# Block-sparse attention, expert attention and an MLP in one kernel: the same instructions in another order of issue, with other PSUM banks

## Chip, core and metric

The kernel runs on one core of one Trainium2 chip. The metric is the device time of one execution in microseconds, lower is better. Every program here computes the same outputs from the same inputs.

## The reference

Three stages follow each other, in fp32. The first is attention on q, k, v of shape (2, 8, 768, 64). Each query sees the keys within 16 positions, and besides them 24 block keys (the maximum over each block of 32 keys) with block values (the mean over the block):

```python
k_sum = k.reshape(B, H, nb, block, D).max(axis=3)
v_sum = v.reshape(B, H, nb, block, D).mean(axis=3)
scores_l = scale * np.matmul(q, k.transpose(0, 1, 3, 2))
mask_l = np.abs(pos[:, None] - pos[None, :]) < window
scores_s = scale * np.einsum('bhsd,bhnd->bhsn', q, k_sum) + np.log(block)
scores_all = np.concatenate([np.where(mask_l, scores_l, -1e9), scores_s], axis=-1)
return softmax(scores_all) @ np.concatenate([v, v_sum], axis=2)
```

Its output, as x of shape (2, 768, 512), goes into a mixer of four experts. Each expert is a causal attention head of width 64 with its own output matrix, and each token adds up its two best experts, weighted by a softmax over their two gate logits:

```python
for e in range(E):
    q, k, v = x @ wq[e], x @ wk[e], x @ wv[e]
    a = softmax(causal(scale * (q @ k.transpose(0, 2, 1))))
    out += gate[e] * (a @ v @ wo[e])
```

The third stage mixes tokens by two matrices of rank 32 and ends with an MLP, 512 to 2048 to 512, and a residual:

```python
u = x + (x.transpose(0, 2, 1) @ U @ V).transpose(0, 2, 1)
return u + np.maximum(u @ w_ch1, 0.0) @ w_ch2
```

## The kernel before

**Tiling.** The 16 heads form eight pairs (numbered 0 to 7), and each pair has three *slots* of 256 queries, 24 slots in all. A slot runs through four steps on TensorE: the scores (L410), the transposes of the exponentials (L421), the weighted sum over V (L433) and the transposes of the result (L448), with VectorE (DVE), ScalarE (ACT) and GpSimd (POOL) between them. For each pair SP loads K (L310), two halves of q (L313) and V (L357). POOL writes scaled copies of K and of the block maxima into the score operands (`kcopy`, L398) and casts the block sums of V into V's tile (`vcast`, L246); DVE takes the maxima over blocks of K (`kmax`, L381); TensorE adds up the blocks of V (`vsum`, L364). There are three q buffers and three V buffers, taken by the pair's number modulo 3, and two K buffers, taken modulo 2. In the rows `ex`, `pt_77` and `w1h_85` are the q buffers 0, 1 and 2; `a_86` holds the raw K; `pt_78` with `c_79` is the score operand 0, `w1h_82` with `w1l_83` the score operand 1; `vb` and `w1l_84` hold V; `vs` are the block sums of V and `ks` the block maxima of K.

The mixer's projections (L594, L645), its scores (L676), its transposes (L709) and its sums (L727) follow, first for batch 0 while attention of batch 1 still runs. The products of the mixer and the MLP are made of three matmuls, of a high and a low part of each operand. The MLP of batch 0 (L961, L974) and of batch 1 (L901, L933) stands at the end, from about 200 us on.

**Warm-up.** 37 matmuls of zeros (`wake_up`, L331) are spread over the beginning: most ahead of the first real work, the others between its steps. Each is recorded as two matmuls in the profile, as are all matmuls of fp32.

**What sets the order.** Nothing of the order is found at run time. Each piece of work (a load, a copy, the scores of a slot, ...) is registered as a *unit* by `at` (L1002), and a unit may have several parts, one after the other (for the scores: the matmuls, then the row minimum on DVE, then the exponentials on ACT). A table `TIMES` (from L48) gives a rank, 0 to 1925, to every part of the 783 units. A loop at the end of the kernel takes the parts by rank and issues their instructions, and each engine, SP's queue of loads among them, works through its own instructions in the order of issue. A second table, `BANKS`, gives a unit the PSUM bank (one of eight) that it writes:

```python
return BANKS[part] if BANKS else i                       # bank_of
...
t, u, i, fn, args = heapq.heappop(todo)
part_now[0] = u
part = fn(*args) if callable(fn) else fn
wait = next(part, None) if isinstance(part, GeneratorType) else None
if wait is not None:
    heapq.heappush(todo, (TIMES[u][i + 1] if TIMES else t + wait, u, i + 1, part, ()))
```

An instruction that has to wait for another engine, or for a buffer or a bank to come free, holds up all that stands behind it on its own engine. On SP this goes for loads into a buffer that is still read: the load, and every load behind it, is issued once the readers are done.

Of the kernel before, what the change touches and what calls it, by code (L numbers as in the profile page):

```python
# [35 lines left out]
def f(ap):  # L36
# [12 lines left out]
    (67,), (107,), (84,), (3,), (52,), (39,), (41,), (80,), (119,), (8,), (42,), (56,), (36,), (220,), (159,), (44,),  # L49
    (179,), (75,), (48,), (106,), (47,), (2,), (1,), (6,), (40,), (477,), (49,), (9,), (22,), (66,), (21,), (76,),  # L50
    (37,), (65,), (74,), (4,), (24,), (138,), (27,), (26,), (16,), (43,), (12,), (14,), (20,), (15,), (57,), (86,),
    (32,), (112,), (0,), (77, 79, 92), (101, 114), (122, 129), (140, 149, 155), (83, 90, 94), (98, 116), (124, 130),
    (139, 144, 165), (89, 91, 109), (110, 111), (127, 143), (148, 164, 167), (113, 115, 126), (128, 142), (154, 166),
    (193, 202, 212), (117, 125, 136), (150, 153), (173, 180), (195, 201, 209), (118, 123, 133), (145, 151),
    (156, 188), (204, 221, 256), (170, 172, 185), (194, 210), (217, 230), (241, 252, 282), (161, 169, 174),
    (183, 198), (229, 250), (251, 258, 293), (176, 184, 190), (200, 205), (228, 254), (275, 284, 302),
    (207, 213, 218), (226, 240), (261, 265), (279, 289, 306), (211, 225, 232), (253, 255), (269, 276),
    (288, 297, 309), (208, 219, 234), (243, 248), (273, 286), (298, 299, 316), (259, 264, 266), (291, 294),
    (304, 313), (333, 340, 354), (263, 267, 281), (287, 292), (301, 325), (335, 336, 356), (277, 290, 305),
    (311, 320), (327, 329), (337, 351, 362), (307, 314, 317), (363, 378), (380, 388), (397, 411, 421),  # L60
    (310, 324, 345), (408, 422), (433, 440), (446, 471, 476), (328, 331, 341), (366, 371), (382, 399),
    (405, 423, 425), (367, 379, 394), (418, 427), (444, 450), (454, 464, 467), (368, 387, 401), (413, 426),
    (445, 453), (455, 463, 473), (376, 384, 389), (415, 432), (435, 457), (533, 534, 549), (430, 438, 451),
    (461, 479), (484, 486), (516, 520, 536), (439, 449, 458), (474, 481), (485, 498), (521, 527, 537),
    (436, 442, 456), (483, 500), (512, 543), (547, 608, 612), (17,), (13,), (58,), (11,), (50,), (23,), (10,), (28,),
    (46,), (19,), (38,), (34,), (29,), (51,), (54,), (55,), (33,), (69,), (18,), (64,), (78, 85, 88), (97,), (104,),
    (103,), (93,), (5,), (7,), (45,), (31,), (30,), (62,), (25,), (53,), (60,), (71,), (61,), (63,), (70,), (59,),
    (87,), (96, 102, 105), (132,), (121,), (35,), (73,), (81,), (72,), (108,), (99,), (134,), (131,), (160,), (137,),
    (146,), (135, 141, 152), (186,), (175,), (82,), (120,), (158,), (100,), (168,), (171,), (182,), (178,), (181,),
    (189,), (197,), (177, 187, 196), (235,), (247,), (147,), (157,), (95,), (162,), (192,), (199,), (223,), (245,),  # L70
    (236,), (216,), (203,), (233, 239, 260), (296,), (280,), (191,), (215,), (231,), (206,), (249,), (283,), (278,),
    (272,), (262,), (285,), (268,), (319, 322, 334), (375,), (364,), (224,), (246,), (271,), (242,), (326,), (312,),
    (365,), (348,), (339,), (330,), (350,), (318, 323, 342), (419,), (385,), (270,), (308,), (355,), (274,), (357,),
    (349,), (400,), (392,), (381,), (343,), (377,), (383, 391, 396), (420,), (424,), (315,), (369,), (410,), (352,),
    (237, 257, 300), (238, 303, 332), (163, 214, 227), (295, 321, 338), (344, 373, 374), (346, 359, 361),
    (390, 395, 402), (347, 353, 360), (358, 370, 372), (386, 393, 398), (403, 404, 407, 412, 414, 417, 429, 431, 493),
    (68,), (406, 409, 416, 434, 437, 459, 469), (428, 441, 443, 447, 448, 465, 470), (222,), (244,), (480, 482, 494),
    (487, 490, 495), (499, 501, 514, 529), (594, 599), (541, 554), (567, 571), (489, 503, 506), (505, 511, 515),
    (522, 535, 550, 551), (556, 557), (502, 513, 517), (492, 507, 525), (526, 552, 564, 566), (574, 577), (572, 580),
    (452, 462, 466, 468, 475, 497, 508), (460, 472, 478, 488, 496, 504, 509), (519, 523, 538), (528, 540, 542),  # L80
# [1181 lines left out]
```

## Time and profile before

| | us |
|---|---|
| median of three runs (428.94, 429.00, 430.14) | 429.0 |
| the profiled execution | 429.18 |
| its span, from the first instruction to the last | 427.4 |
| TensorE busy | 419.6 (98%) |
| DVE busy | 296.1 (69%) |
| ACT busy | 244.8 (57%) |
| POOL busy | 202.9 (47%) |

The busy time of an engine says how much of the span it worked, not who waited for whom. That is to be read from the rows of single stretches: each row has the start of a group of instructions, how long the group took, and in square brackets the idle time before it with what ended that time. PE is TensorE, SPq the queue of SP, which issues the loads. The granted clock of TensorE is 1.00 in all stretches.

### The profile page before, as it was taken

To read this page: it belongs to the slowest core of one execution; us is meant where nothing else is said; L and a number is where in the kernel's file an instruction comes from. 1 tells how busy PE (TensorE), PEld (TensorE's weight loads), DVE (VectorE), ACT (ScalarE), POOL (GpSimd) and SP (SyncE) were. 2 spreads that over 40 slices of the span, in tenths; PEclk is the share of its full clock that TensorE was granted. 3 is DMA by queue.
4 is the path that set the end of the run, shared out by engine and by line. 5 is a ranking of instruction groups with operands and counts; after the bars stand their busy time and mean duration, and the time that the engine had idled before them with its cause. 6 is when DMAs were issued, how large, how long until landed. Compare 5 with 4: busy or idle time off the path is not lost.

```text
span 427.4 us, 9539 instructions
## 1 busy us (share of the span) xinstructions
PE 419.6 (98%) x3594; PEld 386.6 (90%) x3594; DVE 296.1 (69%) x784; ACT 244.8 (57%) x623; POOL 202.9 (47%) x286
## 2 busy tenths in 40 slices
PE   8899999999999999999999999999999999999995
PEld 8789889999989988978888898998889999999995
DVE  4688856776758766669778467666659876755664
ACT  6669856567766778886465453443453554434341
POOL 6799893368785877832254443434543132000000
PEclk9999999999999999999999999999999999999999
DMA  8989850000112013511346234231103000000001
GB/s 215 219 234 248 220 119 2 5 0 20 44 62 64 2 49 100 196 41 61 92 156 200 97 123 123 75 123 51 50 26 123 2 2 0 26 28 0 26 26 49
DMA packets 14925, 35.24 MB, mean 82 GB/s; under 512 B 2080, under 2 KB 3616, under 8 KB 14880
## 3 DMA queue, kind: packets, MB, share of 16 engines
q1 hardware_dynamic: 14880, 34.64, 27.2%
q8 instruction: 28, 0.46, 0.5%
q14 instruction: 17, 0.14, 0.1%
HBM read 31.49 MB, written 3.15 MB: 81 GB/s over the span
## 4 chain that ended last, share of the span: by engine, by line
PE 94%; DMA 2%; SPq 1%; DVE 1%; issue 0%; POOL 0%; DVEq 0%; ACT 0%; POOLq 0%
PE ps L974 16%; PE ps L933 13%; PE ps L901 8%; PE ps L961 8%; PE ps L645 8%; PE ps L524 5%; PE ps L676 5%; PE ps L410 4%; PE ps L594 4%; PE ps L727 4%; PE ps L709 4%; PE ps L983 4%; PE ps L433 3%; PE ps L421 3%; DMA vb<-in_vW_dram 2%; PE ps L448 1%
## 5 line engine op out<-in xcount | busy, mean ns | idle before, releaser
L246 POOL TENSOR_SCALAR a<-a 64x384 fp32r<-64x384 f32 x64 | 33.4, 523 | 19.4 <-ACT a L650 10.2
L966 ACT ACTIVATE a<-ps 128x384 fp32r<-128x384 f32 x32 | 15.6, 491 | 40.2 <-PE ps L961 36.5
L961 PE MATMUL ps<-x,w1h 128*128 128x384 f32 x128 | 37.6, 339 | 0.0
L901 PE MATMUL ps<-x,w1h 128*128 128x256 f32 x192 | 37.2, 282 | 0.0
L645 PE MATMUL ps<-x,m 128*128 128x384 f32 x192 | 37.1, 342 | 0.0
L645 PEld LDWEIGHTS ps<-x,m 128*128 128x128 f32 x192 | 33.0, 188 | 0.1
L968 DVE SCALAR_TENSOR_TENSOR a<-ps,a 128x384 fp32r<-128x384 f32 x32 | 17.7, 553 | 19.9 <-ACT a L966 19.8
L901 PEld LDWEIGHTS ps<-x,w1h 128*128 128x128 f32 x192 | 30.8, 189 | 0.1
L700 POOL TENSOR_SCALAR ex<-ex,rs,gate 128x256 f32<-128x256 f32 (+5 forms) x36 | 24.9, 699 | 6.8 <-DVE nmx L684 2.6
L676 PE MATMUL ps<-a 128*128 128x384 f32 (+4 forms) x128 | 27.7, 337 | 0.0
L687 ACT ACTIVATE ex<-ex,nmx 128x256 f32<-128x256 f32 (+5 forms) x36 | 23.4, 651 | 7.1 <-DVE nmx L684 5.9
L901 PE MATMUL ps<-x,w1l 128*128 128x256 f32 x96 | 27.1, 282 | 0.0
L974 PE MATMUL ps<-m,a 128*128 128x512 f32 x108 | 26.8, 393 | 0.0
L249 DVE TENSOR_TENSOR x<-x,x 128x384 fp32r<-128x384 f32 (+1 forms) x28 | 17.7, 639 | 12.3 <-ACT x L908 9.8
L263 DVE TENSOR_SCALAR x<-x 128x256 uint32<-128x256 uint32 (+3 forms) x38 | 20.3, 541 | 8.0 <-DMA x<-in_w_dram 6.9
L684 DVE CUSTOM_DVE_ANT_0 ex<-ps,cc 128x256 f32<-128x256 f32 (+5 forms) x36 | 20.8, 598 | 6.6 <-PE ps L676 2.7
L267 DVE SCALAR_TENSOR_TENSOR x<-x 128x256 uint32<-128x256 uint32 (+3 forms) x38 | 22.9, 614 | 3.3 <-ACT x L265 3.1
L961 PEld LDWEIGHTS ps<-x,w1h 128*128 128x128 f32 x128 | 23.6, 188 | 1.4 <-issue 0.4
L974 PEld LDWEIGHTS ps<-m,a 128*128 128x128 f32 x108 | 20.0, 188 | 3.7
L265 ACT ACTIVATE x<-x 128x256 f32<-128x256 f32 (+3 forms) x38 | 20.6, 554 | 3.5 <-DMA x<-in_w_dram 3.5
L717 ACT COPY pt<-ps 128x384 f32<-128x384 f32 (+1 forms) x40 | 19.9, 519 | 4.2 <-PE ps L709 4.0
L249 DVE TENSOR_TENSOR a<-a,a 128x384 fp32r<-128x384 f32 (+1 forms) x24 | 15.6, 657 | 8.9 <-ACT a L918 4.8
(317 smaller groups left out, 1236.2 us busy)
## 6 DMA issues: line engine op xcount, KB each, us to landing
x<-in_w_dram SPq DMA_DIRECT2D x16, 512.0 KB, 3.6
x<-in_w_dram SPq DMA_DIRECT2D x20, 256.0 KB, 2.9
vb<-in_vW_dram SPq DMA_DIRECT2D x5, 585.0 KB, 5.8
a<-in_kP_dram SPq DMA_DIRECT2D x7, 416.0 KB, 6.4
out_dram<-a SPq DMA_DIRECT2D x11, 256.0 KB, 2.0
x<-in_wm_dram SPq DMA_DIRECT2D x4, 386.0 KB, 6.2
tb<-in_w_dram SPq DMA_DIRECT2D x6, 256.0 KB, 3.1
a<-in_w_dram SPq DMA_DIRECT2D x6, 256.0 KB, 3.1
```

Of the source, the lines that this page charges most:

```text
L246: pool.tensor_scalar(dst, src, 1.0, 0.0, op0=ALU.mult, op1=ALU.add)
L249: dve.tensor_tensor(dst, src, f(hi), op=ALU.subtract)
L267: dve.scalar_tensor_tensor(low, high, 3, low, op0=ALU.logical_shift_left, op1=ALU.bitwise_or)
L524: pe.matmul(acc, wo[k][:, int(a == 2), 128 * c:128 * c + 128], w[k][:, int(a == 1)], start=j == 0, stop=j == 11)
L645: pe.matmul(acc, (WML if wl else WMH)[k][:, 128 * e:128 * e + 128], xt(b, k, xl)[:, c], start=n == 0, stop=n == 11)
L676: pe.matmul(flat[:, base + c0:base + c1], QS[u][:, 128 * i:128 * i + 128], kk[:, c0:c1], start=x == 0, stop=x == 1)
L687: act.activation(ex[:, 0:W], ex[:, 0:W], AF.Exp, bias=nmx, scale=-1.0, accum_out=sums)
L700: pool.tensor_scalar(ex, ex, rs[:, i % 2:i % 2 + 1], gate[b][:, i, e:e + 1], op0=ALU.mult, op1=ALU.mult)
L901: pe.matmul(acc[:, 256 * i:256 * i + 256], (W1L if wl else W1H)[q][:, c, 128 * (ff % 2):128 * (ff % 2) + 128], cp(1, c, xl)[:, o], start=m ...
L933: pe.matmul(acc[:, 256 * hf:256 * hf + 256], v[:, BLK[a]], w[wl], start=g < 2 and q == 0 and hf == 0 and i == 0, stop=q == 7 and i == 2, s ...
L961: pe.matmul(acc, (W1L if wl else W1H)[ff // 2][:, c, 128 * (ff % 2):128 * (ff % 2) + 128], cp(b, c, xl)[:, o], start=n == 0, stop=n == 5)
L974: pe.matmul(out_bank(b, 3 * j + t), a[:, 128 * t:128 * t + 128], w, start=False, stop=ff == 15 and x == 2, skip_group_check=True)
```

## The change

Only the numbers in the two tables change. The units, their parts, the instructions and the lines of the code are the same; 771 of the 783 entries of `TIMES` have other ranks, and 266 units have another bank. So on each engine the same instructions stand in another order, and the matmuls write other banks.

```diff
 TIMES = [
-    (67,), (107,), (84,), (3,), (52,), (39,), (41,), (80,), (119,), (8,), (42,), (56,), (36,), (220,), (159,), (44,),
...
+    (63,), (42,), (88,), (3,), (32,), (54,), (11,), (39,), (24,), (10,), (22,), (47,), (43,), (189,), (71,), (51,),
...
 BANKS = [
-    -1, -1, -1, -1, 3, 5, 1, 0, 0, 0, 7, 5, 2, 3, 3, 0, 3, 4, 4, 2, 4, -1, -1, -1, -1, -1, -1, -1, -1, -1, -1, -1, -1,
...
+    -1, -1, -1, -1, 0, 1, 3, 6, 3, 2, 3, 3, 0, 2, 1, 5, 7, 5, 7, 6, 6, -1, -1, -1, -1, -1, -1, -1, -1, -1, -1, -1, -1,
```

The start on TensorE, as a difference of the two orders (- before, + now): warm-up matmuls (L331), the block sums of V of pair 0 (L364) and the scores of slot 0 (L410).

```order
@@ -1,9 +1,9 @@
 L1257 UNCONDITIONAL_BRANCH
-L331 MATMUL ps<-vst 128x128 x29
+L331 MATMUL ps<-vst 128x128 x30
+L364 MATMUL ps<-vb,cc 32x128 x12
 L410 MATMUL ps<-pt_78,ex 64x120 x2
 L410 MATMUL ps<-c_79,ex 64x120 x2
...
-L364 MATMUL ps<-vb,cc 32x128 x12
 L331 MATMUL ps<-vst 128x128 x2
```

The block sums of V of pair 0 have moved from behind the scores of slot 0 to ahead of them, and one warm-up matmul from behind them to the start.

The loads on SP before, from the last pieces of pair 0 on. Row 14 is V of pair 1, rows 13 and 11 the last q of pair 0, row 15 the two q halves of pair 1, rows 16 and 20 K of pairs 2 and 3, rows 19 and 22 the two q halves of pair 2, rows 17 and 21 those of pair 3.

```order
12 L357 DMA vb<-in_vW_dram 96x780
13 L313 DMA ex<-in_qT_dram 64x512
14 L357 DMA vb<-in_vW_dram 96x1560
15 L313 DMA pt_77<-in_qT_dram 64x768 x2
16 L310 DMA a_86<-in_kP_dram 128x832
17 L313 DMA ex<-in_qT_dram 64x768
18 L357 DMA w1l_84<-in_vW_dram 96x1560
19 L313 DMA w1h_85<-in_qT_dram 64x768
20 L310 DMA a_86<-in_kP_dram 128x832
21 L313 DMA ex<-in_qT_dram 64x768
22 L313 DMA w1h_85<-in_qT_dram 64x768
23 L357 DMA vb<-in_vW_dram 96x1560
```

The same place of the new order. Row 14 is V of pair 1, rows 13 and 15 the q halves of pair 1, rows 17 and 22 those of pair 2, rows 21 and 23 those of pair 4.

```order
12 L313 DMA ex<-in_qT_dram 64x512
13 L313 DMA pt_77<-in_qT_dram 64x768
14 L357 DMA vb<-in_vW_dram 96x1560
15 L313 DMA pt_77<-in_qT_dram 64x768
16 L310 DMA a_86<-in_kP_dram 128x832
17 L313 DMA w1h_85<-in_qT_dram 64x768
18 L357 DMA w1l_84<-in_vW_dram 96x1560
19 L313 DMA ex<-in_qT_dram 64x768
20 L310 DMA a_86<-in_kP_dram 128x832
21 L313 DMA pt_77<-in_qT_dram 64x768
22 L313 DMA w1h_85<-in_qT_dram 64x768
23 L313 DMA pt_77<-in_qT_dram 64x768
```

A q half of pair 1 now stands ahead of V of pair 1, and a q half of pair 4 ahead of the second q half of pair 2; the second q half of pair 3 (row 21 before) has moved to behind K of pair 4. Further on, both q halves of pair 5 now stand ahead of a load of mixer weights and of V of pairs 5 and 6; before, one of them stood behind V of pair 5 and the other behind K of pair 6.

POOL before, from the first casts of V's block sums (pair 0) on. Rows 30, 35, 37 and 38 are copies for pair 2.

```order
28 L246 TENSOR_SCALAR vb<-vs 24x8x64
29 L246 TENSOR_SCALAR vb<-vs 24x4x64
30 L398 TENSOR_SCALAR pt_78<-a_86 64x12x64
31 L246 TENSOR_SCALAR vb<-vs 24x8x64
32 L246 TENSOR_SCALAR vb<-vs 24x4x64
33 L246 TENSOR_SCALAR w1h_85<-cc 64x768
34 L246 TENSOR_SCALAR vb<-vs 24x12x64
35 L398 TENSOR_SCALAR pt_78<-ks 64x12x24
36 L246 TENSOR_SCALAR vb<-vs 24x12x64
37 L398 TENSOR_SCALAR pt_78<-a_86 64x12x32
38 L398 TENSOR_SCALAR c_79<-a_86 64x12x32
```

The same place of the new order:

```order
27 L246 TENSOR_SCALAR vb<-vs 24x4x64
28 L246 TENSOR_SCALAR vb<-vs 24x8x64
29 L246 TENSOR_SCALAR vb<-vs 24x4x64
30 L246 TENSOR_SCALAR vb<-vs 24x8x64
31 L246 TENSOR_SCALAR w1h_85<-cc 64x768
32 L246 TENSOR_SCALAR vb<-vs 24x12x64
33 L398 TENSOR_SCALAR c_79<-ks 64x12x24
34 L246 TENSOR_SCALAR vb<-vs 24x12x64
35 L398 TENSOR_SCALAR pt_78<-a_86 64x12x32
36 L398 TENSOR_SCALAR pt_78<-ks 64x12x24
37 L398 TENSOR_SCALAR c_79<-a_86 64x12x32
```

All four casts for pair 0 now stand together, with no copy for pair 2 among them, and the first copy for pair 2 is one of the block maxima.

## Rows read from the trace of the kernel before

**Rows 1.** The page: busy time, share and instructions of each engine; the instruction queue.

```profile
PE 419.6 (98%) x3594; PEld 386.6 (90%) x3594; DVE 296.1 (69%) x784; ACT 244.8 (57%) x623; POOL 202.9 (47%) x286
...
q8 instruction: 28, 0.46, 0.5%
```

**Rows 2.** TensorE by stretch: us, busy us (records), granted clock, DMA share, GB/s.

```profile
0.00:60.00 60.00, 56.66 (x897) 1.00 0.89 224
60.00:200.00 140.00, 139.89 (x1235) 1.00 0.15 49
200.00:424.00 224.00, 223.08 (x1466) 1.00 0.19 64
```

**Rows 3.** Chain of waits behind 200 us: start, us, what.

```profile
272.32 1.05 PE ps L961 x6
```

**Rows 4.** Timeline of all engines, first 18 us.

```profile
7.52 0.58 SPq L357 DMA_DIRECT2D vb<-in_vW_dram  x1
...
9.93 0.43 PE L410 MATMUL ps<-pt,ex 128*64 128x120 f32 x4 [0.44 <-ACT pt L341]
...
12.17 0.86 PE L364 MATMUL ps<-vb,cc 96*32 96x128 f32 x24 [1.20 <-issue]
```

**Rows 5.** Timeline of TensorE, 15 to 32 us.

```profile
15.52 0.87 PE L364 MATMUL ps<-vb,cc 96*32 96x128 f32 x24
...
16.81 0.60 PE L421 MATMUL ps<-cc,woh 128*120 128x128 f32 x4
17.25 0.39 PE L331 MATMUL ps<-vst 128*128 128x128 f32 x2
17.47 0.83 PE L421 MATMUL ps<-cc,pt 128*120 128x128 f32 x4
...
20.84 0.71 PE L331 MATMUL ps<-vst 128*128 128x128 f32 x4
21.48 1.15 PE L433 MATMUL ps<-vb,w1h 120*64 120x65 f32 x32
...
27.18 0.49 PE L331 MATMUL ps<-vst 128*128 128x128 f32 x2
27.59 0.43 PE L410 MATMUL ps<-pt,w1h 128*64 128x120 f32 x4
```

**Rows 6.** Timeline of POOL, 10 to 46 us.

```profile
18.87 0.83 POOL L398 TENSOR_SCALAR pt<-a 64x768 f32<-64x768 f32 x1 [2.27 <-DMA a<-in_kP_dram]
...
26.66 0.83 POOL L398 TENSOR_SCALAR c<-a 64x768 f32<-64x768 f32 x1
```

**Rows 7.** Timeline of DVE, first 19 us.

```profile
18.66 0.95 DVE L381 TENSOR_REDUCE ks<-a 128x24 f32<-128x768 f32 x1 [0.85 <-DMA a<-in_kP_dram]
```

**Rows 8.** DMA from 0 to 60 us; loads issued at 18.75, 27.51, 40.49 (KB, us to landing).

```profile
DMA packets 5050, 13.41 MB, mean 224 GB/s; under 512 B 976, under 2 KB 1616, under 8 KB 5040
...
w1h<-in_qT_dram SPq DMA_DIRECT2D x1, 192.0 KB, 7.3
...
a<-in_kP_dram SPq DMA_DIRECT2D x1, 416.0 KB, 4.3
...
w1h<-in_qT_dram SPq DMA_DIRECT2D x1, 192.0 KB, 8.1
```

**Rows 9.** Timeline of TensorE, 32 to 56 us.

```profile
33.85 0.43 PE L410 MATMUL ps<-w1h,ex 128*64 128x120 f32 x4
...
47.34 0.69 PE L433 MATMUL ps<-vb,wol 120*64 120x65 f32 x16
47.86 1.00 PE L433 MATMUL ps<-vb,w1l 120*64 120x65 f32 x16
48.64 0.43 PE L410 MATMUL ps<-w1h,w1h 128*64 128x120 f32 x4
...
53.61 0.37 PE L410 MATMUL ps<-w1l,w1h 128*64 128x120 f32 x2
54.52 0.42 PE L410 MATMUL ps<-w1l,w1h 128*64 128x120 f32 x2 [0.54 <-issue]
```

282 rows, old and new, of tables (BANKS, TIMES) are left out of this document.

## The prediction

> **What bounds the kernel now.** I read the page first: TensorE is busy for 419.6 of 427.4 us, 98% [rows 1]. So a change that issues the same work in another order can win only what TensorE loses now, and the next view asks where that is. The busy time by stretch [rows 2] shows 56.66 of 60 us before 60 us, 139.89 of 140 up to 200 us, and 223.08 of 224 behind that. Third, the chain of waits [rows 3]: from 200 us to the end it is TensorE alone, matmul behind matmul at one spacing; six matmuls of 384 columns take 1.05 us, 175 ns each, wherever they stand. Two things follow. Behind 200 us no order is shorter, since nothing waits there and the last sums and stores stand in the same places in both orders. And what can be won lies in the first 60 us, where a full queue of loads, the K copies on POOL and TensorE take turns in being last. The granted clock is 1.00 in all three stretches [rows 2], so no stretch is slowed by it now, and the new order has TensorE as full as before.
>
> I then went through the first 60 us by the timelines of TensorE, SP, DVE and POOL [rows 4 to 7, 9], asking at each unusual step which engine had ended last. Four places are left, and the sum has one term for each. The profiled execution took 429.18 us, its span 427.4, so 1.8 us lie around the span and stay. It stands 0.18 above the median of the three runs, 429.0; I sum against 429.18 and take the 0.18 off at the end.
>
> **Term 1, up to the first scores of pair 2.** They are at 27.59 now [rows 5]. In the new order three things must be there, and the last decides.
>
> *TensorE itself.* Now it computes scores from 9.93, stands idle for 1.20 us, and takes the V sums of pair 0 at 12.17, when the second V half is there [rows 4]. The new order takes these sums first, so the scores of slot 0 move from that hole to behind 12 us. This is paid out of the next hole: the V sums of pair 1 wait for V of pair 1, issued at 7.52 and used from 15.52 [rows 4, 5]. A q load of 192 KB now stands ahead of this V; at the mean rate of the first 60 us, 224 GB/s [rows 8], that is 0.88 us, so it comes at 16.40. From 15.52 to 27.59 are 12.07 us. Out of these goes the transpose of a slot, moved ahead of the sums (0.44, from 16.81 to 17.25), and one warm-up matmul, moved likewise (0.22, from 17.25 to 17.47) [rows 5]. That gives 16.40 + 12.07 - 0.66 = 27.81. Two warm-up stretches last longer than their matmuls: four records take 0.64 us from 20.84 and two take 0.41 from 27.18, where 0.44 and 0.22 would do [rows 5]; what follows them was late. The new order moves a score slot and a weighted sum ahead of these places, so I take these 0.39 us as gone: 27.42.
>
> *POOL.* Now TensorE starts the scores right behind POOL's copy of 26.66, which ends at 27.49. Before this, POOL stood idle for 2.27 us at 18.87 because a copy of K of pair 2 was ahead in its order, and K had not landed. From there to 27.49 it ran 12 instructions without a hole, 8.62 us, 0.72 each [rows 6]. The new order puts the four V casts of pair 0 into this hole; behind the maxima over K, which end at 18.66 + 0.95 = 19.61 [rows 7], eight instructions are left: 19.61 + 8 x 0.72 = 25.4. If the hole goes somewhere else, before the casts, the bound is the old 27.49. POOL is no longer last.
>
> *The q of pair 2.* Its second half now stands behind a q of pair 4, and that one is written where pair 1's q lies, so SP waits for the last scores of pair 1. This is the wait that the change adds: queued behind it on SP are q of pair 2, another q of pair 4, V and K. Those scores end by 20.84 now [rows 5]; the V of pair 1 adds 0.88 and takes back 0.66, and a transpose and a weighted sum go ahead (about 0.44 + 0.52), so 22.0. The q of pair 2 is then issued at about 22.5. How long it takes to land is not shown for this place: the nearest rows are 4.3 us for 416 KB issued behind a pause of four microseconds, and 7.3 us for this very load at its old place in a full queue [rows 8]. SP issues little in the microseconds before 22, so the row with the pause is nearer: 26.8. At 7.3 it is 29.8.
>
> So TensorE is last, at 27.42: **-0.2 us**. The bounds: 26.5 if every wait inside goes, -1.1 (the records from 15.52 on, each at the spacing of its kind, need 10.7 of the 12.07 us); 29.8 by the slow landing, +2.2.
>
> **Term 2, warm-up matmuls.** Of 37, 29 stand ahead of the first real work now and 30 after. The one that goes from behind the scores of pair 3 saves 0.22 where TensorE paces itself: **-0.2**, or 0 if the next step waits anyway.
>
> **Term 3, the q of pair 5.** Issued at 40.5, it needs 8.1 us [rows 8], and the scores at 48.64 are its reader: the 16 matmuls before them take 0.78 us to the next row, those of 47.34 take 0.52 [rows 9]. In the new order both q loads of pair 5 stand ahead of a mixer weight and two V loads instead of behind the K of pair 6, so they are there in time: **-0.26**, at the least 0.
>
> **Term 4, the pause in the scores at 53.61.** Two matmuls, then 0.91 us to the next row where 0.1 would do, and the profile calls the releaser "issue" [rows 9]: no semaphore. I read it as TensorE's instructions being fetched late in a full DMA queue; the instruction queue moved 0.46 MB in 28 packets [rows 1]. In the new order other loads stand at that time, so it may go, stay or move: 0 to -0.8, and I take half, **-0.4**.
>
> **What costs nothing.** The q of pair 3 that was issued at 18.2 now stands behind K of pair 4, which is issued when POOL's last copy for pair 2 is done, at 27.5 now. At 28.0 plus the 4.3 us of [rows 8] it lands at 32.3, ahead of its scores at 33.85 [rows 9]; with 1.5 us of cover lost it would be in the way. The four splits of mixer weights on POOL now stand together, behind copies that the scores wait for. The PSUM banks: by the order, the nearest two uses of one bank in the attention part now have more matmuls between them than before; in the mixer some stand nearer together, most of all in its last rows. I price that at 0, since no wait on a bank stands among the steps read above; one that came free too late would show as a TensorE wait of some tenths.
>
> **The sum.** -0.2 - 0.2 - 0.26 - 0.4 = -1.06 against 429.18, that is 428.1, and 427.9 against the median. Of runs of this kernel about 0.3%, 1.3 us, can be told from no change.
>
> **Where a rule speaks otherwise.** TensorE's busy share is 98% and its weight loads' 90% [rows 1]. The Trainium skill, "Perfetto Trace Analysis", section "Identifying the Most-Contended Engine", says that the busy share of matmuls is a bad measure of how close a kernel is to its limit, since matmuls are pipelined, and that the share of weight loads should be used. By this 10%, some 41 us, would be open. The trace does not bear it out as something an order can win: the spacing of 175 ns is the same through the whole second half [rows 3], with no wait between.
>
> **Rivals.**
> *A, the forecast*, 427.9, by the four terms; between 426.9 and 428.9 as terms 1 and 4 come out.
> *B, loads and POOL pace the first 55 us whatever TensorE's order is.* For it: K of pair 2 lands when it lands, both orders move the same bytes ahead of it, and what TensorE saves is waited for at the next load. Against it: the scores of pairs 3 and 4 do not wait now. All terms vanish: 429.0.
> *C, slower: the added SP wait.* The q of pair 2 is issued at 22.5 and lands with the 7.3 us of its old place. It decides from a landing time of 4.9 us on, 27.42 - 22.5. At 7.3 the scores of pair 2 begin at 29.8, 2.2 us late instead of 0.2 early, and nothing gives it back since TensorE is full from there: 427.9 + 2.4 = 430.3; the q of pair 3, queued further back on SP, can add some tenths. For it: two of the three loads in [rows 8] took over 7 us. Against it: the queue drains meanwhile.
> *D, larger gain.* Term 1 at its bound (-1.1) and term 4 whole (-0.8): -2.4, 426.6, and less if holes too small for a row go too.
> *E, open weight-load time can be won by order*, by the rule above: under 425, with a spacing below 175 ns.
>
> **How the numbers follow.** A 0.48, B 0.17, C 0.20, D 0.13, E 0.02. The predicted time is A's, 427.9. Faster by over 0.3% means under 427.7: D, E and a little under half of A (0.23), 0.38. Slower means over 430.3: of C 0.16, since it is priced at its edge and can only grow by queued loads. Same is the rest, 0.46. The range holds all of A and B, D down to 425.8 and C up to 430.8; what it leaves out is E, the tails of C and D.
>
> **What would show it.** Right: the V sums of pair 0 ahead of all scores at about 11.8 us; POOL's hole at 18.87 gone and its last copy for pair 2 before 26.5; the scores of pair 2 at 27.0 to 27.6; no step of 1.00 us before the scores of pair 5; spacing of 175 ns behind 200 us, and the last matmul about 1 us earlier. Wrong: scores of pair 2 behind 28 us, with a wait for a q load (C); a TensorE wait for DVE or ACT behind 100 us, which would say that a bank is written again too soon; or a granted clock below 1.00 in some stretch.

## The result: slower, by 1 to 4 us

Beside runs of the kernel before, the changed kernel took 433.5 us (median of 6) against 429.4: ratio 1.0062, 95% interval 1.0035 to 1.0090. Run a second time, in 12 executions, it took 431.1 against 430.1: 1.0023 (0.9997 to 1.0049). A ratio here is estimated together with its interval and is not the quotient of the two medians, which for the first measurement is 1.0095. Medians and ratios leave out executions over 1.5% above the fastest of their kernel: one of the kernel before, and seven in three of the kernels below. The forecast was 427.9 with a range of 425.8 to 430.8, so it had the wrong sign, and both medians lie above the range; the second measurement alone would not rule out that nothing changed. The new order also spreads more: 428.4 to 434.5 over the 18 executions, where the kernel before mostly stays between 428.5 and 431.

The profiled execution of the changed kernel took 433.75 us, 4.57 more than that of the kernel before (429.18). The page of the changed kernel, its busy times and its granted clock in 40 slices:

```profile
PE 419.8 (97%) x3594; PEld 387.3 (90%) x3594; DVE 298.2 (69%) x784; ACT 245.6 (57%) x623; POOL 205.7 (48%) x286
...
PEclk9899999999999999999999999999999999999999
```

TensorE's busy time is the same [rows 1]; one slice, the second, is no longer at full clock. By stretch, as in [rows 2]:

```profile
0.00:60.00 60.00, 52.16 (x857) 0.97 0.83 206
60.00:200.00 140.00, 139.96 (x1251) 1.00 0.17 50
200.00:428.00 228.00, 227.63 (x1492) 1.00 0.20 68
```

TensorE is busy for 52.16 of the first 60 us, where it was 56.66: 4.50 us less, all but 0.07 of the difference (time at half clock counts as busy here). From 60 us on it has nothing to wait for. So the new order and the new banks behind 60 us cost nothing, and the spacing behind 200 us is the old one, 1.06 us for the six matmuls of [rows 3]:

```profile
311.82 1.06 PE ps L961 x6
```

TensorE's waits, by what ended them (us in total, times, longest):

```profile
PE ps L364 <- DMA vb<-in_vW_dram: 3.9, 1, 3.9
PE ps L410 <- issue: 1.9, 2, 1.5
PE ps L331 <- DVE vst L327: 1.1, 1, 1.1
PE ps L410 <- DMA ex<-in_qT_dram: 1.0, 1, 1.0
```

Three are new or longer: for V of pair 0, for a q load, and two pauses with no releaser ("issue"). In order of time:

**The start.** TensorE's timeline, and its clock by stretch:

```profile
13.28 0.87 PE L364 MATMUL ps<-vb,cc 96*32 96x128 f32 x24 [3.90 <-DMA vb<-in_vW_dram]
14.07 0.62 PE L410 MATMUL ps<-pt,ex 128*64 128x120 f32 x4
14.47 0.62 PE L410 MATMUL ps<-c,ex 128*64 128x120 f32 x4
...
17.71 0.37 PE L410 MATMUL ps<-pt,ex 128*64 128x120 f32 x4
17.92 0.37 PE L410 MATMUL ps<-c,ex 128*64 128x120 f32 x4
```

```profile
9.40:13.20 3.80, 0.00 (x0) 1.00 1.02 218
...
14.10:17.40 3.30, 3.30 (x27) 0.51 1.00 208
17.40:20.00 2.60, 2.60 (x45) 0.96 1.09 231
```

The V sums now come first, and their second half of V landed at 13.19 (12.08 in the kernel before). TensorE stood idle for 3.90 us. The first V sums still ran at full clock; from 14.1 to 17.4 the granted clock is 0.51, that is 1.2 instead of 2.4 GHz, and four score records take 0.40 us from row to row (14.07 to 14.47) instead of 0.21 (17.71 to 17.92).

**POOL.** What the V casts wait for, on ACT and on POOL:

```profile
16.62 1.11 ACT L416 ACTIVATE woh<-ps,nmx 128x120 f32<-128x120 f32 x4 [6.62 <-DVE nmx L413]
17.76 0.29 ACT L341 COPY w1h<-a 64x120 f32<-64x120 f32 x1
18.06 0.25 ACT L369 COPY vs<-ps 24x128 f32<-24x128 f32 x1
```

```profile
20.13 2.24 POOL L246 TENSOR_SCALAR vb<-vs 24x256 f32<-24x256 f32 x4 [3.24 <-DVE w1l L1015]
...
29.71 0.83 POOL L398 TENSOR_SCALAR c<-a 64x768 f32<-64x768 f32 x1
```

The V sums are first on TensorE, but their copy (L369) stands behind the exponentials of slot 0 on ACT and the additions behind two row minima on DVE. They were done on TensorE at 14.1; POOL got them at 20.13, after a hole of 3.24 us where the old hole was 2.27 [rows 6]. The row at 29.71 is POOL's last copy for pair 2.

**The q of pair 3.** The loads on SP, and their way to TensorE:

```profile
30.57 0.35 SPq L310 DMA_DIRECT2D a<-in_kP_dram  x1
30.97 0.47 SPq L313 DMA_DIRECT2D ex<-in_qT_dram  x1
```

```profile
30.77 0.38 PE L410 MATMUL ps<-pt,w1h 128*64 128x120 f32 x4
...
38.17 0.43 PE L410 MATMUL ps<-w1h,ex 128*64 128x120 f32 x4 [1.01 <-DMA ex<-in_qT_dram]
...
44.65 0.43 PE L410 MATMUL ps<-pt,pt 128*64 128x120 f32 x4
46.59 0.42 PE L410 MATMUL ps<-c,pt 128*64 128x120 f32 x4 [1.51 <-issue]
```

The row at 30.77 is the first scores of pair 2 (27.59 before, [rows 5]). K of pair 4 waits for POOL's last copy for pair 2, which now ends at 30.54 instead of 27.49; the q of pair 3 is queued behind it, lands at 38.03, and its scores stand for 1.01 us. **Late instructions.** The pause at 46.59 is of the same kind as that of [rows 9] at 54.52: in the middle of one slot's scores, with no semaphore.

### The profile page after: what moved, and what is told of

It reads as the page before. It is cut to its first block, busy times and chain, and to the rows that moved or that the text cites. A ratio compares the mean times of both kernels' runs of the same rounds, so it can differ in the third digit from the quotient of the medians.

```text
span 432.0 us, 9539 instructions
## 1 busy us (share of the span) xinstructions
PE 419.8 (97%) x3594; PEld 387.3 (90%) x3594; DVE 298.2 (69%) x784; ACT 245.6 (57%) x623; POOL 205.7 (48%) x286
## 4 chain that ended last, share of the span: by engine, by line
PE 93%; DMA 3%; SPq 1%; issue 1%; DVE 1%; ACT 0%; POOL 0%; DVEq 0%
PE ps L974 15%; PE ps L933 13%; PE ps L901 8%; PE ps L645 8%; PE ps L961 8%; PE ps L524 5%; PE ps L676 5%; PE ps L410 5%; PE ps L727 4%; PE ps L709 4%; PE ps L594 4%; PE ps L983 4%; PE ps L433 2%; PE ps L421 2%; DMA vb<-in_vW_dram 2%; DMA ex<-in_qT_dram 2%
## 5 line engine op out<-in xcount | busy, mean ns | idle before, releaser
L700 POOL TENSOR_SCALAR ex<-ex,rs,gate 128x256 f32<-128x256 f32 (+5 forms) x36 | 26.3, 738 | 7.5 <-DVE rs L695 2.4
L267 DVE SCALAR_TENSOR_TENSOR x<-x 128x256 uint32<-128x256 uint32 (+3 forms) x38 | 27.1, 731 | 3.1 <-ACT x L265 2.9
L413 DVE TENSOR_REDUCE nmx<-ps 128x4 f32<-128x480 f32 x24 | 15.4, 653 | 11.8 <-PE ps L410 11.3
L961 PE MATMUL ps<-x,w1l 128*128 128x384 f32 x64 | 21.6, 338 | 0.0
L676 PEld LDWEIGHTS ps<-a 128*128 128x128 f32 x128 | 20.2, 189 | 1.0 <-issue 0.3
```

Of the source, the lines that this page charges most:

```text
L267: dve.scalar_tensor_tensor(low, high, 3, low, op0=ALU.logical_shift_left, op1=ALU.bitwise_or)
L676: pe.matmul(flat[:, base + c0:base + c1], QS[u][:, 128 * i:128 * i + 128], kk[:, c0:c1], start=x == 0, stop=x == 1)
L700: pool.tensor_scalar(ex, ex, rs[:, i % 2:i % 2 + 1], gate[b][:, i, e:e + 1], op0=ALU.mult, op1=ALU.mult)
L961: pe.matmul(acc, (W1L if wl else W1H)[ff // 2][:, c, 128 * (ff % 2):128 * (ff % 2) + 128], cp(b, c, xl)[:, o], start=n == 0, stop=n == 5)
```

## Experiments

Changes of the tables are shown in terms of the parts in their order of issue (a number behind a name is the pair, or the slot of scores; then the half). Times are medians; the ratio to the kernel before, run beside it on the same chip, carries the interval. All kernels below compute everything.

**Which stretch.** The first 96 parts of the order, to about 16 us, as before, with the banks of before for them:

```diff
-parts 0..95 in the new order
+parts 0..95 in the order of before
 all other parts in the new order
```

> Only the first 96 parts (to the V sums of pair 1, about 16 us) as before, all later ones in the new order. Theory: the start alone (V sums first, 3.9 us idle, then half the clock) costs 3 of the 4 us, and the wait for the q of pair 3 (1.0) and the pauses without a releaser (1.1 more than before) stay: 430.5 (429.7 to 431.5). Rival: loads pace the first 40 us, and what the start wins is waited for again at the q of pair 3: 432.5 to 433.5.

Measured 429.4 against 429.7: 0.9994 (0.9979 to 1.0008). More than the 3 us came back: all of it. As far as the interval tells, the rest of the new order is as good as the old one. The start of this kernel, TensorE's timeline and clock:

```profile
10.36 0.43 PE L410 MATMUL ps<-pt,ex 128*64 128x120 f32 x4
...
11.33 0.87 PE L364 MATMUL ps<-vb,cc 96*32 96x128 f32 x24
12.12 0.71 PE L331 MATMUL ps<-vst 128*128 128x128 f32 x4
```

```profile
9.40:13.20 3.80, 3.80 (x62) 1.00 1.02 251
13.20:18.00 4.80, 4.80 (x78) 1.00 0.88 228
```

The scores fill the time until V is there, and nothing stands. The wait for the q of pair 3 has shrunk to 0.3 us, and the pause at matmul 596 is gone, though nothing of those places was changed.

A longer piece, 344 parts to about 57 us:

```diff
-parts 0..343 in the new order
+parts 0..343 in the order of before
 all other parts in the new order
```

> The first 344 parts (to about 57 us) in the order and banks of the kernel before, all later parts in the new order with the new banks. Theory: everything that the new order loses lies in the first 60 us, so this runs like the kernel before, 429.0 (428.4 to 430.0). Rival: the later order or the new banks cost part of it; then 431 or more, with TensorE waits for DVE or ACT behind 60 us.

Measured 431.4: 1.0050 (1.0027 to 1.0074), slower than either order. The cause is the seam:

```profile
56.71 1.66 PE L594 MATMUL ps<-m,x 128*128 128x260 f32 x8 [1.58 <-ACT ex L416]
```

The mixer's first projection waits 1.58 us for ACT, where the two orders do not fit together, and behind this wait the granted clock is 0.50 from 57.30 to 60.70. Of the question it was made for, the time decides nothing; the profile has no wait of TensorE behind the seam.

The reverse, the start of the new order ahead of the old one:

```diff
-parts 0..93 in the order of before
+parts 0..93 in the new order
 all other parts in the order of before
```

> The reverse of the kernel whose start was as before: the first 94 parts (to the V sums of pair 1) in the new order with the new banks, all later parts in the order and banks of before. Theory: the start alone is the loss: 432 (431 to 433), a spread of 3 us or more. Rival: the start is only half of it and needs the new loads behind it (q of pair 3 behind K of pair 4) to be felt: 430 to 430.5.

Measured 431.0 against 430.1: 1.0035 (1.0008 to 1.0062), from 429.9 to 435.0. The new start alone makes the old kernel slower and spreads it, by about 1 us in the median (1.5 by the ratio) and not 2. In its profile, of 433.3 us, the granted clock is 0.50 from 12.10 to 18.80, and the scores of pair 2 begin at 31.52.

**The changed kernel again.**

> The changed kernel once more, unchanged, beside the kernel before on the same chip. Theory: V of pair 0 lands anywhere from 11.4 to 13.2 us with this one sequence of loads, and the new order, in which TensorE has nothing else until then, passes this on: times spread over 429 to 435, with a median of 431 to 433. Rival: the loss is a fixed 4 us: 433 to 434 with a spread of less than 2.

Measured 431.1, 428.4 to 433.2, ratio above. The rival of a fixed 4 us has fallen. In this execution V was there earlier:

```profile
12.00 0.86 PE L364 MATMUL ps<-vb,cc 96*32 96x128 f32 x24 [2.34 <-issue]
12.79 0.43 PE L410 MATMUL ps<-pt,ex 128*64 128x120 f32 x4
```

2.34 us idle, and the clock stayed up. From there this execution ran nearly as forecast: POOL's last copy for pair 2 ended at 27.70, and the scores of pair 2 began at 27.93 (30.77 in the first profile, 27.42 in the forecast). What it lost, it lost later. The q of pair 3, issued at 28.13, took 7.3 us to land, its scores stood for 1.20 us, and there was a pause at matmul 596 (the table below):

```profile
ex<-in_qT_dram SPq DMA_DIRECT2D x1, 192.0 KB, 7.3
```

```profile
35.53 0.43 PE L410 MATMUL ps<-w1h,ex 128*64 128x120 f32 x4 [1.20 <-DMA ex<-in_qT_dram]
```

With this sequence of loads the second V half landed anywhere from 11.4 to 13.2 us in ten profiled executions (with the sequence of before 10.8 to 12.3 in eight). A kernel that has put nothing else in front of V passes this on. Since the changed kernel itself is 1 to 4 us slower, no kernel below is held against its 433.5; all go by their ratio to the kernel before.

**Parts of the start.** The loads alone, back in their old sequence up to the q of pair 1:

```diff
 load order on SP:
-ident, K0, K0, mask, mask, K1, q0, pick, q0, V0, V0, q0, q0, q1, V1, q1
+mask, ident, K0, mask, K0, V0, q0, q0, K1, pick, q0, V0, q0, V1, q1, q1
```

> The new order with the first loads (all up to q of pair 1) in the sequence of the kernel before on SP; TensorE, ACT, DVE and POOL stay in the new order, the V sums first. Theory: the loads' sequence makes V of pair 0 late (13.2 against 12.1 or less before): it lands at 11 to 12 us, the idle time ahead of the V sums falls from 3.9 to 2 to 2.5 us, the clock stays up, and 2 of the 4 us come back: 431.5 or less. Rival: the V sums in front are the loss, whatever the loads: 433.

Measured 431.6: 1.0037 (1.0017 to 1.0056). The idle time fell to 1.53 us and the clock stayed up, but only in part for the reason that the theory gave: V landed at 12.32, 0.87 us earlier than in the first profile of the changed kernel, and the warm-up matmuls ended at 10.88 instead of 9.38 us, since TensorE ran them at six or seven records per us until 7 us, where in the changed kernel it reached eleven at 4 us. The time hardly came back: the waits for the q of pair 3 (1.4) and at matmul 596 are there as before.

The scores of slot 0 ahead of the V sums again, with the q load they need:

```diff
+load_q(0, 0)
 load_v(0)
-load_q(0, 0)
...
+a_scores(0)
 vsum(0)
-a_scores(0)
```

> The new order with the scores of slot 0 ahead of the V sums of pair 0, as before, and the one q load that they need ahead of V. Theory: the scores fill the hole in front of the V sums, the clock stays at 1.00 from 14 to 17 us, everything up to the scores of pair 2 comes 1.5 to 2.5 us earlier: 431 to 432, since the q of pair 3 and the late instructions are still there. Rival: the loss is made by the loads behind the start (q of pair 3 behind K of pair 4), as moving that one load alone suggests: 433, with the same wait at the q of pair 3.

Measured 430.5: 1.0014 (0.9992 to 1.0037). In the range; no longer distinguishable from the kernel before. In the profile the pause at matmul 596 is 2 us, and behind it the granted clock is 0.50 from 44.50 to 47.90.

Only ACT and DVE, the V sums' copy and additions ahead of slot 0's softmax:

```diff
 vsum(0) on TensorE
+vsum(0): copy on ACT, additions on DVE
 a_scores(0): row minimum, exponentials
-vsum(0): copy on ACT, additions on DVE
```

> The new order with the ACT copy and the DVE additions of the V sums of pair 0 moved ahead of the row minimum and the exponentials of slot 0 (they stand behind them in the new order). TensorE, POOL and the loads stay in the new order. Theory: POOL's V casts wait at 20.13 us only for these, so POOL runs 3 us earlier, the last copy for pair 2 is done at 27.5 instead of 30.5, K of pair 4 and the q of pair 3 behind it are issued 3 us earlier, and the 1.0 us wait at 38.17 goes although the start is as slow as in the new order: 431 to 432. Rival: POOL has slack there and the late V sums on TensorE are all that counts: 433.5.

Measured 430.2: 1.0018 (0.9994 to 1.0041). In the profile POOL's casts start at 15.4, K of pair 4 is issued at 27.2, the q of pair 3 lands at 33.4, and no scores wait for it: the chain is as the theory says. Its price is not settled, as the intervals of this kernel and of the unchanged one overlap.

The V sums first in the kernel before:

```diff
+vsum(0) on TensorE
 a_scores(0) on TensorE
-vsum(0) on TensorE
 (order of before)
```

> The kernel before with one step moved: the V sums of pair 0 ahead of the scores of slot 0 on TensorE; loads, ACT, DVE and POOL as before. Theory: the idle time moves to the front of the V sums (9.3 to 11 or 12 us), 0.9 us of scores is paid behind it, and V of pair 1 at 15 us and POOL behind it hide most of that, since ACT and DVE still take the V sums when they come: 429.7 to 430.2. Rival: V sums first is the loss by itself, 431 or more.

Measured 430.9 against 430.1: 1.0021 (0.9997 to 1.0044). More than I expected, and just short of certain. The profile does not put the loss at the start alone: the scores of pair 2 begin at 28.05, 0.46 us later than before, and further on TensorE waits 0.6 us for the q of pair 5 and, at 179.10, 1.2 us for DVE in the scores of the mixer.

**The clock.** 17 more warm-up matmuls in the hole:

```diff
-WAKE = (10, 4, 3) + (2,) * 6 + (1,) * 8
+WAKE = (27, 4, 3) + (2,) * 6 + (1,) * 8
```

> The new order with 17 more warm-up matmuls ahead of the first V sums, so that TensorE does not stand idle while it waits for V of pair 0. Nothing else changes, and the V sums cannot start earlier. Theory: half the clock from 14.1 to 17.4 us costs 1.9 us of its own beside the wait: 431.6, granted clock 1.00 throughout. Rival: only the wait counts, and the load of V of pair 1 or the q of pair 3 is the next to be late in any case: 433 to 433.5 though the clock is full.

Measured 432.6, from 429.3 to 439.0: 1.0059 (1.0027 to 1.0090). In the profile the warm-up matmuls lasted until 13.59, beyond V's landing at 11.91, so the run does not answer cleanly. The clock stayed full at the start, the scores of pair 2 came 1.2 us earlier than in the changed kernel, and this was lost again: the q of pair 3 was waited for (1.1), matmul 597 came 3.3 us after the one before it, and behind that the granted clock was 0.50 from 45.90 to 49.30.

**The loads behind the start.** One q load moved:

```diff
 load_q(4, 0)
+load_q(3, 0)
 load_v(3)
 load_k(4)
-load_q(3, 0)
```

> The new order with one load moved: the second q half of pair 3 ahead of V of pair 3 and K of pair 4, right behind the q of pair 4, instead of behind K of pair 4. Theory: the 1.0 us wait at 38.17 goes: 432.5 (and no TensorE wait for a q load). Rival: the other loads move back by as much, and K of pair 4 or the instructions come later instead: 433.5.

Measured 430.1: 1.0017 (0.9996 to 1.0037). The wait for the q of pair 3 is gone, and the pause at 596 too. And the same load moved the other way, in the kernel before:

```diff
-load_q(3, 0)
 load_v(3)
 load_k(4)
+load_q(3, 0)
 (order of before)
```

> The kernel before with one load moved: the second q half of pair 3 from ahead of V of pair 3 to behind K of pair 4, as in the new order. Theory: K of pair 4 is issued at 26.5 to 27.5 when POOL's last copy for pair 2 is done, the q lands 6 to 7 us behind it, at 33.5 to 35, and its scores at 33.85 wait in most executions: 430.3 to 431.0, with a wait of 0.5 to 1.5 us at the scores of slot 9. Rival, as the prediction had it: it lands at 32.3, no cost, 429.7.

Measured 430.1 against 429.95: 1.0002 (0.9990 to 1.0015). The theory fell, and the rival, which is the prediction's "costs nothing", holds here. The row of the load (KB, us to landing), issued at 27.54, and its reader:

```profile
ex<-in_qT_dram SPq DMA_DIRECT2D x1, 192.0 KB, 5.7
```

```profile
33.49 0.43 PE L410 MATMUL ps<-w1h,ex 128*64 128x120 f32 x4
```

It landed at 33.19, 0.30 us ahead of its scores. So the place behind K of pair 4 costs nothing in the old order, where the load lands in 5.7 us, and has almost no cover left. In the new order, where the same load took 7.1 and 7.3 us in the two profiles, it costs 1.01 and 1.20.

**Instructions.** Three mixer weights moved back:

```diff
-moe_weights(1), moe_weights(2)
 load_q(5, 1), load_q(5, 0)
-moe_weights(0)
 load_v(5)
+moe_weights(1), moe_weights(2), moe_weights(0)
```

> The new order with the loads of three mixer weights moved from ahead of the q of pair 5 to behind V of pair 5 (their splits on ACT move back too). Theory: the pause of 1.5 us in the scores at 46.59 comes from TensorE's instructions being fetched behind a queue of 2 MB that was issued from 35.3 to 37.9; with 1.2 MB less in it the fetch is in time and the pause goes: 432. Rival: the pause has nothing to do with the loads: 433.5 and the same pause at the same matmul.

Measured 430.6: 1.0029 (1.0009 to 1.0049). The pause at matmul 596 is gone. What the pauses hang on shows in all profiles together. TensorE's instructions come in packets of 16 KB on a queue of their own (the 28 packets of [rows 1]), through the same DMA engines as the loads. In the changed kernel the fourth starts at 43.78; the instruction queue's row of the window from 43.7 to 43.9 us is (packets, MB, share of the 16 DMA engines)

```profile
q8 instruction: 1, 0.02, 40.4%
```

Times in us, from the packets' and matmuls' records (matmuls counted from 0):

| kernel | packet 4 starts | matmul 596 starts | step before it | after the packet |
|---|---|---|---|---|
| changed kernel | 43.78 | 46.59 | 1.78 | 2.81 |
| changed kernel again | 40.23 | 43.13 | 0.96 | 2.90 |
| old loads | 41.56 | 44.54 | 1.46 | 2.98 |
| scores first | 41.02 | 43.75 | 2.05 | 2.74 |
| start of before | 37.80 | 40.91 | no pause | 3.11 |
| weights later | 37.81 | 41.08 | no pause | 3.27 |
| kernel before | 35.80 | 41.28 | no pause | 5.48 |

Wherever TensorE pauses in this table, it goes on 2.7 to 3.0 us after the packet has begun, and where the packet is earlier there is no pause. The sixth packet does the same at matmul 849 to 852: 2.2 to 2.6 us after it in the kernel before, in the changed one and in eleven others. In the kernels with 17 and with 8 more warm-up matmuls, which are 34 and 16 more records, the pause stands at matmul 597 and 596 all the same, in V sums and in transposes: it goes with the count of the instructions and not with the work. By that count (7188 matmuls and weight loads in 28 packets) a packet holds about 128 matmuls, so I measure the delay of the fourth from matmul 468. It starts 4.2 to 5.4 us behind that matmul in the four kernels of the table that pause, and 1.3 to 3.3 us behind it in the other three. What makes a packet late is not shown: the DMA engines are as full ahead of it in the kernel before (share 1.08 from 34.50 to 35.80) as in the changed one (1.05 from 38.70 to 43.80). In the changed kernel nine loads, of about 3150 KB together, were issued from 30.57 to 37.89, ahead of packet 4.

**Mended.** The last three cures together, V sums still first:

```diff
 new order
+load_q(3, 0) ahead of load_v(3)
+moe_weights(1), (2), (0) behind load_v(5)
+vsum(0): copy and additions ahead of a_scores(0): row minimum
```

> The new order with three moves: the q of pair 3 ahead of V of pair 3; three mixer weights behind V of pair 5; the ACT copy and DVE additions of the V sums of pair 0 ahead of the row minimum and exponentials of slot 0. TensorE still takes the V sums first. Theory: only the hole in front of the V sums is left, 0.5 to 1 us: 429.8 to 430.4 beside 429.7 of the kernel before. Rival: V sums first cost nothing once POOL is in time: 429.2 or less. Second rival: the waits are not those three: 431.

Measured 431.7 against 429.95: 1.0027 (1.0014 to 1.0040). The second rival comes nearest, and the profile has the start again (TensorE's row, then its clock by stretch):

```profile
12.28 1.50 PE L364 MATMUL ps<-vb,cc 96*32 96x128 f32 x24 [2.25 <-issue]
```

```profile
10.00:12.20 2.20, 0.02 (x1) 0.98 1.10 219
12.20:15.40 3.20, 3.12 (x40) 0.50 1.04 227
15.40:18.00 2.60, 2.60 (x39) 0.98 1.03 231
```

So the three later waits are not the whole loss. They come with the start, since they shrank or went when only the first 96 parts were as before; but mending them leaves the late start and its half clock. Then 8 more warm-up matmuls, which end before V lands, in this kernel and in the changed one:

```diff
-WAKE = (10, 4, 3) + (2,) * 6 + (1,) * 8
+WAKE = (18, 4, 3) + (2,) * 6 + (1,) * 8
```

> The kernel with the three loads and copies mended (V sums still first) with 8 more warm-up matmuls ahead of the V sums, 1.8 us that end before V of pair 0 lands. Theory: the clock stays at full speed in (nearly) every execution, mean granted clock 0.997 or more, and the 1.5 us that an execution with half the clock loses are gone: 430.0 to 430.6 against 431.7. Rival: waiting for V is the loss, and the clock only shows it: 431.7 as before.

> The changed kernel with the same 8 more warm-up matmuls and nothing else. Theory: no execution with half the clock, 430.5 to 431 instead of 431 to 433.5, and the wait for the q of pair 3 and the late fetch at the 596th matmul (604th with these) remain. Rival: with TensorE earlier it meets these two waits earlier and they give the gain back: 431.5 or more, at full clock.

Measured 431.6: 1.0049 (1.0025 to 1.0072), and 433.0: 1.0071 (1.0047 to 1.0096). Both theories fell and both rivals held, though the clock stayed up in 10 of 12 and 6 of 8 executions. In the profile of the second, the wait for the q of pair 3 (0.7) and pauses at matmuls 596 and 849 (1.9 and 1.4) remain. In that of the first, the scores of pair 3 came at 33.99, 2.1 us earlier than without the warm-ups, and then TensorE and POOL show this:

```profile
37.31 0.69 PE L433 MATMUL ps<-w1l,w1h 120*64 120x65 f32 x16 [1.46 <-POOL w1l L246]
```

```profile
35.25 0.51 POOL L398 TENSOR_SCALAR c<-a 64x384 f32<-64x384 f32 x1 [3.01 <-DMA a<-in_kP_dram]
```

POOL stands 3 us for K of pair 4, and a V cast that TensorE needs is queued behind that copy. What the full clock gained was waited for again.

**A kernel better than both?** The start of before with the q of pair 3 earlier, and this with the weights later:

```diff
 parts 0..95 in the order of before, all others in the new order
+load_q(3, 0) ahead of load_v(3)
```

> The new order with the start of before (first 96 parts) and the second q half of pair 3 ahead of V of pair 3 and K of pair 4. Theory: the wait of 0.3 for the q of pair 3 goes and the executions in which it is longer are no longer there: 429.0 (428.5 to 429.4), lower than the 429.44 with the start of before alone. Rival: POOL's copies are as late as the q, no gain: 429.4.

```diff
 the kernel above
+moe_weights(1), (2), (0) behind load_v(5)
```

> The new order with the start of before (96 parts), the q of pair 3 ahead of V of pair 3 and the three mixer weights behind V of pair 5. Theory: with loads spread so the instruction fetches are in time, the pause of 1.0 us at the 849th matmul shrinks: 428.6, against 429.2 without the mixer weights moved. Rival: the weights stand in the queue when the next fetch comes, or ACT and POOL wait for them ahead of the mixer: 429.2 to 429.6.

Measured 429.2 against 430.1: 0.9983 (0.9966 to 1.0001), and 430.1 against 429.95: 0.9996 (0.9984 to 1.0008). The first is the best kernel of the study, by an interval that just includes no gain; the second lost this again, with waits for ACT, V and the q, and the pause at matmul 849 did not shrink (1.12 us against 0.99).

## Why the prediction was wrong, step by step

**Term 1, TensorE.** This is the step that failed, in three places. I let V of pair 1 (16.40) be the next thing late, and took the scores' old hole to be paid out of the wait for it. In the first profile the second V half came at 13.19, where the sum rested on about 11.8; the scores of slots 0 to 2 ran behind it, most of them at half clock, and the sums of pair 1 began at 19.84, not at 16.40, though V of pair 1 was there at 17.76. I put the clock at nothing, since TensorE was to be "as full as before": it stood idle for 3.90 us and then ran for 3.30 us at 0.51, which by my estimate from these rows lost 1.6 us of work. And I asked only when TensorE gets to the V sums, not who hands them on: their ACT copy and DVE additions had moved behind slot 0's softmax, which no order of TensorE or POOL shows. The scores of pair 2 began at 30.77; predicted was 27.42. In the second profile, with V at 11.91 and a full clock, they began at 27.93. So the swap as such need not cost; what failed is that I took one landing time as fixed and left TensorE nothing else to do until then.

**Term 1, POOL.** "POOL is no longer last" took the casts as ready for POOL's old hole, which ended at 18.87. In the first profile they were not (20.13), POOL's last copy for pair 2 ended at 30.54 instead of before 26.5, and with it K of pair 4 slipped by 3 us; in the second they came at 17.40 and that copy ended at 27.70.

**Term 1, the q of pair 2, and rival C.** The added wait on SP is there, the q was issued at 26.13 and not at 22.5, but it landed in 3.4 us, at 29.53, ahead of its scores. C had the sign and, at 430.3, nearly the lower of the two times, by a mechanism that did not decide. The low landing time, 4.3 by the row behind a pause, was even too high.

**Term 2.** One warm-up matmul less behind the start: nothing that a wait would not swallow. No run measured it.

**Term 3** held: both q loads of pair 5 landed by 46.97, and their scores at 52.60 wait for nothing.

**Term 4**: the reading was right (instructions fetched late), the price had the wrong sign. I took half of 0.8 as gone; the pause moved and grew, 1.78 us at matmul 596 and 0.64 at 849 against 0.80 before.

**What costs nothing.** The q of pair 3 did cost, 1.01 us in the first profile and 1.20 in the second. A late POOL is not the whole reason, since in the second its last copy for pair 2 ended only 0.21 us later than before. The landing time was mis-sized: I took the 4.3 us of a load behind a pause, and it was 7.1 and 7.3 us, behind three q loads, V and K issued in the 5.4 us before it. In the kernel before, with the same load moved, it was 5.7 us and cost nothing. I had named the cover, 1.5 us, and joined it neither to that queue nor to term 1. The banks at nothing and the stretch behind 200 us were right. The weight loads' 90%, rival E, bought nothing: spacing 175 ns as before.

**B**, that loads and POOL pace the first 55 us whatever TensorE does, describes what the experiments met again and again: half a dozen cures of one wait made the next load, cast or fetch the late one. It was priced at no change because I looked at what TensorE could save, not at what a late start would set off.

**What is shown and what is open.** Shown: the loss is made by the first 96 parts, by their order or their banks (no wait on a bank shows); with these as before, three kernels stand at 0.9994, 0.9983 and 0.9996, and the new start ahead of the old order stands at 1.0035. Shown in single profiles: of the nine with the V sums first and without more warm-ups, the scores of pair 2 begin at 29.68 to 31.52 us in the four in which the clock fell there, and at 27.43 to 28.67 in the five in which it did not. V came at 12.19 to 13.19 in the four and at 11.35 to 12.32 in the five, so a late V and a low clock are not told apart by this. Shown: no cure of one later wait, and not three together, brings the changed kernel level with the kernel before beyond doubt. Open: how the loss divides among the V sums first, the loads' sequence and the late copy. Each cure of a part moved the ratio to between 1.0014 and 1.0037, with intervals that overlap each other and that of the kernel unchanged (1.0023).

## What to carry to other kernels

An order is not better because each engine has fewer holes in it: ask what the first item of an engine waits for, how much that landing time varies, and what else could run there. When a step moves on one engine, follow its result through every engine that hands it on; here the matmuls moved to the front and their copy to the back. A load that has 0.3 us of cover is free only as long as nothing ahead of it slips, so price such loads together with the term that could slip, not alone, and take the landing time from a row with a like queue ahead of it.

## What the runs showed of the hardware

**The clock fell in some executions of the same kernel and not in others.** Half the clock followed idle times of 3.90, 3.45, 2.50 and 2.25 us ahead of the V sums, and not 2.34, 2.00, 1.99, 1.70 or 1.53, so the length alone does not decide near 2.3. It also followed later waits of 3.01, 1.79 and 1.58 us (the kernels with 17 more warm-ups, with the scores first and with 344 parts as before), and not waits of 1.51 us (the changed kernel) and 1.58 us (with 8 more warm-ups). In the nine measurements with the V sums first and without more warm-ups, 33 of 97 executions have a mean granted clock of 0.996 or less, with a median of 432.1 us; the other 64 have 430.6. Of the kernel before it is 5 in 148. Where in an execution the clock fell is known of the profiled ones alone. Yet the warm-ups, which kept the clock up, did not bring the 1.5 us back, so this difference need not be the clock's: a late V comes with it.

**Instruction fetches can be late while loads are queued.** A packet of 16 KB lets a TensorE that waits for it go on only 2.2 to 3.0 us after it starts, and in the changed kernel the fourth started 5 us after TensorE had passed matmul 468 (38.70 to 43.78 us), against 1.3 us in the kernel before (34.52 to 35.80). The Trainium skill, "Runtime: NRT & Kernel Launch", section "Instruction fetch mechanics", says that instructions come in blocks of 16 KiB, 256 instructions, over a DMA queue that the sequencer drives, and that the cost of crossing a block is mostly hidden. The packets' size agrees; the cost is not always hidden: pauses of 0.6 to 3.3 us at matmul 596 or 597, or at 849 to 852, stand in 15 of the 19 profiles here.

**The landing of one load varies by 1.8 us** from execution to execution with nothing changed ahead of it (11.4 to 13.2 us for the second V half).
